# Residual by accumulating DMA, convolution in groups of eight, output stages by time

## The chip, the cores and the metric

The kernel runs on one core of a Trainium2 chip, as one launch. The metric is device time in microseconds, from the first to the last instruction; lower is better. A core has a matrix engine (PE, whose weight loads the profile lists apart as PEld), a vector engine (DVE), a scalar engine (ACT), a general engine (POOL), and SyncE (SP), which here only issues DMAs. POOL issues DMAs as well. PE writes to PSUM, which is cut into banks; DVE and ACT read PSUM and the on-chip memory SBUF; DMAs move data between SBUF and the main memory (HBM).

## The reference, cut to what matters

Two operations in a row: a depthwise convolution over seven past tokens, whose weights are a softmax for each of eight heads, and then a token-mixing block with a phase.

```python
# x: (8, 4224, 192); weight: (8, 7)
w = softmax(weight, axis=-1)
x = causal convolution of x along the tokens, w[h] for the 24 channels of head h

theta = x @ w_theta                       # 192 x 192
zr, zi = x * cos(theta), x * sin(theta)
yr = einsum('ts,bsd->btd', w_tok_r, zr)   # 4224 x 4224, mixes the tokens
yi = einsum('ts,bsd->btd', w_tok_i, zi)   # 4224 x 4224
u = x + yr + yi                           # the residual: x is the convolution's output
return u + np.maximum(u @ w_ch, 0.0)      # 192 x 192
```

## The kernel before

The tokens are 33 chunks `k` of 128 tokens on the input side of the token mixing, and 33 blocks `tb` of 128 tokens on its output side. A row holds batch times channel: N = 8 x 192 = 1536 elements.

**Steps.** The work on PE is a list of 58 steps. A step takes a pair of output blocks (the last unit has one block only) and at most NW = 11 chunks that are in SBUF as `z`. The two real products of a pair are done with seven matrix products instead of eight (sums and differences of weights and of `z` prepared by DVE). NU = 17 units of blocks pass by for each group of chunks, and partial sums go to `part` in HBM and come back 17 steps later. In the last 17 steps (`final`) the sum of a block is complete: the residual is added, and the output stage follows. In the last five of them, fewer than eleven chunks are left, so these steps are short.

```python
    # one step: seven runs over the chunks, two matmuls of 384 columns each time
    for r, (wn, zn, cn, opens, to) in enumerate(runs):
        if opens:
            y[cn] = ypool.tile([P, 2, PC], F32, name="y", tag="y")   # two PSUM buffers
        for c, k in enumerate(self.ks):
            while events and events[0][0] * len(runs) <= 7 * (r + c / self.n):
                events.pop(0)[1]()            # other work, placed in sevenths of the step
            yield k
            for q in range(2):
                pe(nc.tensor.matmul(y[cn][:, q, 0:BH], lhsT=..., rhs=chunks[k].z[...], ...))
        if to:
            self.give(y[cn], *to)             # DVE: pv += y
```

Every instruction of PE, DVE and ACT is kept in the order in which the program gives it.

**The convolution** of a chunk is four calls of `conv`, each for two heads: four matmuls into one PSUM bank (tile `pc`), which ACT copies into `z`. While the first eleven chunks are made, the calls stand in twos; afterwards each of them is an event of its own inside a step. Twenty-two chunks are made in that second way.

```python
        def conv(self, hp):
            ...
            pc = bank("pc")                   # one of four banks shared with v and tp
            for hh in range(2):
                h = 2 * hp + hh
                for half in range(2):
                    pe(nc.tensor.matmul(pc[half * 2 * Q : (half + 1) * 2 * Q, ...],
                        lhsT=bands[:, h, :, :]..., rhs=self.xw[:, half, :, ...]))
            act(nc.scalar.activation(out=self.x..., in_=pc[...], func=AT.Copy))
            # after the last call: DMAs of x, as f16 rows, to xs in HBM

        def tasks(self):
            for hp in range(4):
                yield lambda hp=hp: self.conv(hp)
            # then 2 transposes, 4 theta stages, 2 products, 2 sums
    ...
                # sevenths of the step for the tasks of one chunk
                pos = [0, .2, .4, .6, 1.3, 1.5, 2.1, 2.3, 2.5, 2.7, 3.1, 3.15, 3.4, 3.6]
```

**The residual** of a final step is loaded from `xs` and added by DVE to the partial sum `pv` in the step before.

```python
        def load_rows(self):
            for tb in self.tbs:
                pv = wk.tile([P, N], F32, name="pv", tag="big", bufs=6)
                if not self.first:
                    nc.sync.dma_start(out=pv, in_=part[(self.t // NU - 1) % 2][tb, :, :])
                self.pv.append(pv)

        def residual(self, i):
            xr = wk.tile([P, N], F16, name="xr", tag="xr", bufs=1)
            nc.sync.dma_start(out=xr, in_=xs[self.tbs[i] * P : (self.tbs[i] + 1) * P, :])
            dve(nc.vector.tensor_tensor(out=self.pv[i], in0=self.pv[i], in1=xr, op=ALU.add))
    ...
                    found.append((3.7 + 2.3 * i, lambda i=i: steps[t + 1].residual(i)))
```

**The output stage** of a block: ACT casts `pv` to f16 (`ub`), PE transposes it in two halves of six tiles (`tp`), ACT copies each half (`uT`), PE multiplies with `w_ch` (`v`, four times four matmuls), DVE does the maximum and the addition in place, and two DMAs take the result out. All of it stands in the next step, at places counted in sevenths of that step, whatever its length; after the last step it follows at once.

```python
        def outputs(self):
            for i in range(len(self.tbs)):
                at = 0.2 + 3.4 * i
                found.append((at, lambda i=i: self.cast(i)))          # 128 x 1536
                for g in range(NG):
                    found.append((at + 0.8 + 1.0 * g, lambda g=g: self.turn_u(g)))
                    for k in range(2):
                        found.append((at + 1.3 + 1.0 * g + 0.2 * k,
                                      lambda i=i, g=g, k=k: self.output(i, g, k)))
```

Of the kernel before, what the change touches and what calls it, by code (L numbers as in the profile page):

```python
# [9 lines left out]
AT = mybir.ActivationFunctionType  # L10
ALU = mybir.AluOpType
F16 = mybir.dt.float16
# [4 lines left out]
def kernel(  # L17
# [23 lines left out]
    nc = tc.nc  # L41
    B, S, D = x.shape
    H, KS = weight.shape
    G = D // H
    P = nc.NUM_PARTITIONS
    assert (B, D, P) == (8, 192, 128) and S % P == 0
    N = B * D
    HD = D // 2
    HN = N // 2
    NQ = 4  # L50
    Q = P // NQ
# [3 lines left out]
    WR = Q + HALO  # L55
    GB = 4
    NG = B // GB
    GC = GB * D
    BH = HN // 2
    NU = (NT + 1) // 2  # L60
    NW = 11
# [5 lines left out]
    NSTEP = start[-1] + NU  # L67
# [7 lines left out]
    def in_order(engine, ins):  # L75
        if engine in last:
            tc.add_manual_dep(ins.ins, last[engine].ins.name, NOSYNC, reason="order")
        last[engine] = ins
        return ins
# [4 lines left out]
    def dve(ins):  # L84
        return in_order("dve", ins)

    def act(ins):
        return in_order("act", ins)

    constp = ctx.enter_context(tc.tile_pool(name="const", bufs=1))  # L90
    wk = ctx.enter_context(tc.tile_pool(name="wk", bufs=2))
# [11 lines left out]
    xs = dram.tile([S, N], F16, name="xs")  # L103
    part = [dram.tile([NT, P, N], F32, name=f"part{i}") for i in range(2)]
# [26 lines left out]
    def channel_mix(tT, k, w):  # L131
        v = bank("v")
        for b in range(2):
            for i in range(2):
                pe(nc.tensor.matmul(  # L135
                    v[:, b * D : (b + 1) * D], lhsT=tT[:, 3 * k + b + i, :],
                    rhs=w[:, 2 * b + i, :], start=(i == 0), stop=(i == 1),
                ))
        return v[:, 0 : 2 * D]

    def transposed(u):
        tp = bank("tp", F16)
        for k in range(6):
            pe(nc.tensor.transpose(  # L144
                tp[:, k * P : (k + 1) * P], u[:, k * P : (k + 1) * P], ident
            ))
        uT = wk.tile([P, 6, P], F16, name="uT", tag="uT")
        act(nc.scalar.activation(  # L148
            out=uT[:, :, :].rearrange("p k s -> p (k s)"), in_=tp[:, 0 : 6 * P],
            func=AT.Copy,  # L150
        ))
        return uT
# [3 lines left out]
    class Chunk:  # L156
# [83 lines left out]

        def tasks(self):

            for hp in range(4):
                yield lambda hp=hp: self.conv(hp)
            for g in range(NG):
                yield lambda g=g: self.transpose(g)
            for g in range(NG):
                for k in range(2):
                    yield lambda g=g, k=k: self.theta(g, k)
            yield lambda: self.product(Z11)  # L250
            yield lambda: self.product(Z21)
            yield lambda: self.sums(0)
            yield lambda: self.sums(1)
# [13 lines left out]
    class Step:  # L267


        def __init__(self, t):  # L270
            self.t, self.u, self.ks = t, unit(t), active(t)
            self.n = len(self.ks)
            self.tbs = [tb for tb in (2 * self.u, 2 * self.u + 1) if tb < NT]
            self.pair = len(self.tbs) == 2
            self.first = t < NU
            self.final = t + NU >= NSTEP
            self.blocks = ("11", "21", "22", "12") if self.pair else ("11", "12")
            self.st, self.w, self.pv, self.xr = {}, {}, [], []

        def load_w(self, name):  # L280
            tb = self.tbs[int(name[0]) - 1]
# [52 lines left out]
                    )  # L334
                self.pv.append(pv)

        def residual(self, i):
            xr = wk.tile([P, N], F16, name="xr", tag="xr", bufs=1)
            nc.sync.dma_start(
                out=xr, in_=xs[self.tbs[i] * P : (self.tbs[i] + 1) * P, :]  # L340
            )
            dve(nc.vector.tensor_tensor(  # L342
                out=self.pv[i], in0=self.pv[i], in1=xr, op=ALU.add
            ))

        def give(self, y, i, h, copies):
            o = self.pv[i][:, :].rearrange(
# [55 lines left out]
                        out=part[(self.t // NU) % 2][tb, :, :], in_=self.pv[i]  # L403
                    )

        def cast(self, i):
            self.ub = wk.tile([P, N], F16, name="ub", tag="ub", bufs=1)
            act(nc.scalar.activation(out=self.ub, in_=self.pv[i], func=AT.Copy))  # L408

        def turn_u(self, g):  # L410
            self.uT = transposed(self.ub[:, g * GC : (g + 1) * GC])

        def output(self, i, g, k):
            pk = self.pv[i][:, g * GC + k * 2 * D : g * GC + (k + 1) * 2 * D]
            dve(nc.vector.scalar_tensor_tensor(  # L415
                out=pk, in0=channel_mix(self.uT, k, wch), scalar=0.0, in1=pk,
                op0=ALU.max, op1=ALU.add,
            ))
            if k == 1:
                rows = slice(self.tbs[i] * P, (self.tbs[i] + 1) * P)  # L420
                nc.sync.dma_start(
                    out=out[g * GB : (g + 1) * GB, rows, :].rearrange("b s d -> s b d"),
                    in_=self.pv[i][:, g * GC : (g + 1) * GC].rearrange(
                        "p (b d) -> p b d", d=D
                    ),
                )

        def outputs(self):
            found = []
            for i in range(len(self.tbs)):  # L430
                at = 0.2 + 3.4 * i
                found.append((at, lambda i=i: self.cast(i)))
                for g in range(NG):
                    found.append((at + 0.8 + 1.0 * g, lambda g=g: self.turn_u(g)))
                    for k in range(2):
                        found.append((at + 1.3 + 1.0 * g + 0.2 * k,
                                      lambda i=i, g=g, k=k: self.output(i, g, k)))
            return found

    steps = [Step(t) for t in range(NSTEP)]  # L440

    def step_events(t):
        found = []
        s = steps[t]
        if t + 1 < NSTEP:
            found += steps[t + 1].w_tasks()
            found.append((1.6, steps[t + 1].load_rows))
            if steps[t + 1].final:
                for i in range(len(steps[t + 1].tbs)):
                    found.append((3.7 + 2.3 * i, lambda i=i: steps[t + 1].residual(i)))  # L450
        if t + 2 < NSTEP:
            nxt = steps[t + 2]
            for j, name in enumerate(nxt.blocks):
                found.append(((0.3, 1.3, 2.3, 4.3)[j], lambda name=name: nxt.load_w(name)))
        if t > 0 and steps[t - 1].final:
            found += steps[t - 1].outputs()
        if t >= NU - 2:
            new = [k for k in range(NK) if start[k] == t + 2 and k >= NW]
            for k in new:
                found.append((4.5, lambda k=k: load_chunk(k)))  # L460
            at = 0.3
            for k in (k for k in range(NK) if start[k] == t + 1 and k >= NW):
                pos = [0, .2, .4, .6, 1.3, 1.5, 2.1, 2.3, 2.5, 2.7, 3.1, 3.15, 3.4, 3.6]

                def add(at, j, k):
                    def go():
                        if j == 0:
                            chunks[k].todo = chunks[k].tasks()
                        next(chunks[k].todo)()
                    found.append((at, go))  # L470
                for j, p in enumerate(pos):
                    add(at + p, j, k)
                at += 2.6
        return found
# [3 lines left out]
    spare = bank("spare")  # L478
    noise = zpool.tile([P, PC], F16, name="noise", tag="z")
    nc.vector.memset(noise, 0.0)  # L480
    masks = wk.tile([2 * WR, KS, 2, Q], F16, name="masks", tag="ub", bufs=1)
    nc.gpsimd.memset(masks, 1.0)
    for k in range(KS):
        nc.gpsimd.affine_select(
            out=masks[:, k, :, :], in_=masks[:, k, :, :], pattern=[[WR, 2], [1, Q]],
# [5 lines left out]
    for a, lo in ((0, True), (1, False)):  # L491
        nc.gpsimd.affine_select(
            out=block[:, a : a + 1], in_=block[:, a : a + 1], pattern=[[0, 1]],
# [6 lines left out]
        out=wsb, in0=wsb, in1=wmax[:, :].unsqueeze(2).to_broadcast([P, H, KS]),  # L500
        op=ALU.subtract,
# [10 lines left out]
        out=wbf, in0=wsb, in1=wrcp[:, :].unsqueeze(2).to_broadcast([P, H, KS]),  # L512
        op=ALU.mult,
# [2 lines left out]
    nc.vector.tensor_tensor(  # L516
        out=taps, in0=masks[:, :, 0, :], in1=masks[:, :, 1, :], op=ALU.add
    )
    btmp = wk.tile([2 * WR, 2, H, Q], F16, name="btmp", tag="xr", bufs=1)
    for k in range(KS):  # L520
        nc.vector.tensor_tensor(
            out=btmp[:, 1 if k else 0],
            in0=taps[:, k, :].unsqueeze(1).to_broadcast([2 * WR, H, Q]),
            in1=wbf[0 : 2 * WR, :, k].unsqueeze(2).to_broadcast([2 * WR, H, Q]),
            op=ALU.mult,
        )
        if k:
            nc.vector.tensor_tensor(
                out=btmp[:, 0], in0=btmp[:, 0], in1=btmp[:, 1], op=ALU.add
            )  # L530
    for a in range(2):
        nc.vector.tensor_scalar_mul(
            out=bands[:, :, a, :], in0=btmp[:, 0], scalar1=block[:, a : a + 1]
# [77 lines left out]
    wch = channel_weights(moe_w_ch, "wch")  # L611
    ready[0] = NK
    for _ in flow:
        pass
    for _, f in sorted(steps[-1].outputs(), key=lambda e: e[0]):
        f()


# [28 lines left out]
```

## Time and profile before

| | |
|---|---|
| time, median of 3 runs | 1490.7 us (1489.43 to 1496.38) |
| PE busy | 1448.0 us, 97% |
| DVE busy | 1034.9 us, 69% |
| ACT busy | 387.1 us, 26% |
| POOL busy | 566.9 us, 38% |
| moved by DMA | 268.99 MB, mean 180 GB/s |

How to read it: busy time is the union of the times in which an engine executes. Matmuls overlap in their pipeline, so the mean duration of one (327 ns for the large ones) is longer than the distance between the starts of two; how fast PE goes is read from starts, not from durations. A group's line gives the source line, engine, operation, the program's names, the shapes and the count, then busy time and mean ns, then the idle time of that engine just before, with what ended it. A line of the view by stages gives for a stretch its length, each engine's busy time and count of instructions, the granted clock of PE, the DMA share and GB/s.

The trace has five stretches: up to about 110 us the first eleven chunks are made; to 425 us there are steps alone; to 585 us the second eleven chunks are made beside the steps; to 880 us steps alone; to 1042 us the third eleven chunks; from there to the end are the final steps with their output stages.

### The profile page before, as it was taken

The page shows a single profiled execution, that of the slowest core. Times are in us where ns is not written, and L with a number is a line of the kernel's source. Part 1 is how long each engine was busy: PE and PEld are TensorE (multiplying, and loading weights), DVE is VectorE, ACT ScalarE, POOL GpSimd, SP SyncE. Part 2 cuts the span into 40 slices and gives each one's busy share as a digit, 9 for nine tenths or more (in the row PEclk, how much of TensorE's full clock was granted, in tenths as well). Part 3 has the DMA queues.
Part 4 walks back from the last instruction along what each step waited for, and adds up shares of the span by engine and source line. Part 5 has one row for each costly group of instructions (what it writes and reads, how often), then busy time and mean ns, then how long its engine had stood idle before and what let it go on. Part 6 is the DMA issues. An engine that isn't in the chain of part 4 may idle for free.

```text
span 1490.7 us, 25284 instructions
## 1 busy us (share of the span) xinstructions
PE 1448.0 (97%) x10083; PEld 899.1 (60%) x10083; DVE 1034.9 (69%) x1153; ACT 387.1 (26%) x631; POOL 566.9 (38%) x1054
## 2 busy tenths in 40 slices
PE   7899999999999999999999999998999999999996
PEld 3565666666665566666666656565666666666664
DVE  5884554545458777766657568778887787787885
ACT  6881101010134353000000025255112212121233
POOL 9753433332444542433333354442422322232320
PEclk9999999999999999999999999999999999999998
DMA  9996756565799998887878699999787887787783
GB/s 132 234 199 142 142 112 132 109 136 103 166 200 233 223 208 250 195 183 184 187 177 194 169 191 201 231 214 252 144 195 177 186 183 192 184 185 179 173 214 109
DMA packets 240023, 268.99 MB, mean 180 GB/s; under 512 B 76192, under 2 KB 209312, under 8 KB 239904
## 3 DMA queue, kind: packets, MB, share of 16 engines
q0 software_dynamic: 167232, 85.25, 46.9%
q1 hardware_dynamic: 72672, 182.12, 35.0%
q8 instruction: 79, 1.29, 0.3%
q14 instruction: 40, 0.33, 0.1%
HBM read 245.49 MB, written 101.06 MB: 232 GB/s over the span
## 4 chain that ended last, share of the span: by engine, by line
PE 86%; DMA 6%; POOL 3%; DVE 3%; issue 1%; ACT 1%; DVEq 0%; POOLq 0%; ACTq 0%
PE y L389 77%; PE v L135 5%; PE tp L144 2%; POOL st L287 2%; DMA st<-in_moe_w_tok_i_dram 2%; PE pc L190 2%; DMA xw<-in_x_dram 2%; DMA st<-in_moe_w_tok_r_dram 1%; DVE pv L354 1%; POOL xw L177 1%; DVE wt L299 1%; DMA xr<-xs 1%; DVE z L237 1%; DVE z L231 0%; ACT uT L148 0%
## 5 line engine op out<-in xcount | busy, mean ns | idle before, releaser
L389 PE MATMUL y<-z,wt 128*128 128x384 f16 x7656 | 1320.5, 327 | 17.1 <-DVE pv L354 12.0
L389 PEld LDWEIGHTS <-wt 128*128 128x128 f16 x7656 | 734.4, 98 | 473.9 <-issue 22.3
L354 DVE TENSOR_TENSOR pv<-y,pv 128x768 f32<-128x768 f32 x324 | 308.3, 952 | 362.4 <-PE y L389 361.7
L287 POOL DMA_DIRECT2D st<-in_moe_w_tok_r_dram x448 | 241.6, 548 | 425.9 <-DVE wt L299 390.8
L287 POOL DMA_DIRECT2D st<-in_moe_w_tok_i_dram x448 | 242.0, 549 | 404.5 <-DVE wt L299 366.5
L299 DVE STREAM_TRANSPOSE wt<-st 128x1408 f16<-128x1408 f16 (+7 forms) x224 | 326.5, 1462 | 10.0 <-DMA st<-in_moe_w_tok_r_dram 7.4
L148 ACT ACTIVATE uT<-tp 128x768 f16<-128x768 f16 x132 | 106.1, 818 | 330.3 <-PE tp L144 330.3
L311 DVE TENSOR_TENSOR wt<-wt 128x1408 f16<-128x1408 f16 (+7 forms) x216 | 173.4, 803 | 10.1 <-PE y L389 6.6
L197 ACT ACTIVATE z<-pc 128x384 f16<-128x384 f32 x132 | 63.3, 507 | 391.3 <-PE pc L190 390.2
L352 ACT ACTIVATE pv<-y 128x768 f32<-128x768 f32 x66 | 53.8, 817 | 275.6 <-PE y L389 274.7
L135 PEld LDWEIGHTS <-uT 128*128 128x128 f16 x1056 | 93.7, 99 | 40.8 <-ACT uT L148 9.9
L415 DVE SCALAR_TENSOR_TENSOR pv<-v,pv 128x384 f32<-128x384 f32 x132 | 71.2, 548 | 50.0 <-PE v L135 49.5
L177 POOL DMA_DIRECT2D xw<-in_x_dram x132 | 77.1, 602 | 38.8 <-DMA st<-in_moe_w_tok_r_dram 14.9
L226 ACT ACTIVATE z<-v,half_pi 128x384 f16<-128x384 f32 x132 | 77.8, 589 | 31.1 <-PE v L135 30.1
L237 DVE TENSOR_TENSOR z<-z 128x768 f16<-128x768 f16 x132 | 73.6, 557 | 4.8
L135 PE MATMUL v<-wch,uT 128*128 128x192 f16 x528 | 66.0, 251 | 6.4 <-ACT uT L148 6.4
L408 ACT ACTIVATE ub<-pv 128x1536 f16<-128x1536 f32 x33 | 48.8, 1480 | 65.9 <-DVE pv L354 65.9
L226 ACT ACTIVATE z<-v 128x384 f16<-128x384 f32 x132 | 65.5, 496 | 0.0
L231 DVE TENSOR_TENSOR z<-z 128x1536 f16<-128x1536 f16 x66 | 59.9, 949 | 7.7 <-ACT z L226 7.7
L135 PE MATMUL v<-wth,uT 128*128 128x192 f16 x528 | 61.8, 246 | 0.8 <-ACT z L226 0.8
L342 DVE TENSOR_TENSOR pv<-pv,xr 128x1536 f32<-128x1536 f32 x33 | 57.7, 1750 | 2.7 <-DMA xr<-xs 2.7
L190 PE MATMUL pc<-xw,bands 96*64 96x192 f16 x528 | 43.7, 256 | 3.3 <-DMA xw<-in_x_dram 2.8
(44 smaller groups left out, 180.3 us busy)
## 6 DMA issues: line engine op xcount, KB each, us to landing
part<-pv SPq DMA_DIRECT2D x79, 768.0 KB, 4.1
pv<-part SPq DMA_DIRECT2D x79, 768.0 KB, 5.8
out_dram<-pv SPq DMA_DIRECT2D x66, 384.0 KB, 3.9
st<-in_moe_w_tok_r_dram POOLq DMA_DIRECT2D x280, 88.0 KB, 4.9
st<-in_moe_w_tok_i_dram POOLq DMA_DIRECT2D x280, 88.0 KB, 3.4
xs<-z SPq DMA_DIRECT2D x132, 96.0 KB, 3.9
xr<-xs SPq DMA_DIRECT2D x33, 384.0 KB, 4.1
xw<-in_x_dram POOLq DMA_DIRECT2D x121, 96.0 KB, 4.9
```

Of the source, the lines that this page charges most:

```text
L135: pe(nc.tensor.matmul(v[:, b * D : (b + 1) * D], lhsT=tT[:, 3 * k + b + i, :], rhs=w[:, 2 * b + i, :], start=(i == 0), stop=(i == 1),))
L148: act(nc.scalar.activation(out=uT[:, :, :].rearrange("p k s -> p (k s)"), in_=tp[:, 0 : 6 * P], func=AT.Copy,))
L177: nc.gpsimd.dma_start(out=self.xw[lo : lo + n, h, :, :], in_=x[:, t0 : t0 + n, :].rearrange("b s d -> s b d"),)
L190: pe(nc.tensor.matmul(pc[half * 2 * Q : (half + 1) * 2 * Q, hh * B * G : (hh + 1) * B * G], lhsT=bands[:, h, :, :].rearrange("p a m -> p ( ...
L226: act(nc.scalar.activation(**args))
L237: dve(nc.vector.tensor_tensor(out=z[:, o, :], in0=z[:, a, :], in1=z[:, b, :], op=ALU.subtract))
L287: nc.gpsimd.dma_start(out=st[a * Q : (a + 1) * Q, :, 0:n], in_=w[tb * P : (tb + 1) * P, t0 : t0 + n] .rearrange("(bt i) s -> i bt s", bt=NQ),)
L299: dve(nc.vector.transpose(self.w[name][:, 0 : self.n, :, :], self.st[name][:, :, 0 : self.n * Q] .rearrange("p bt (c j) -> p c bt j", j=Q),))
L311: dve(nc.vector.tensor_tensor(out=self.w[name][:, 0 : self.n, :, :], in0=self.w[a][:, 0 : self.n, :, :], in1=self.w[b][:, 0 : self.n, :, : ...
L354: dve(nc.vector.tensor_tensor(out=o, in0=yv, in1=o, op=ALU.add))
L389: pe(nc.tensor.matmul(y[cn][:, q, 0:BH], lhsT=self.w[wn][:, c, :, :].rearrange("p bt i -> p (bt i)"), rhs=chunks[k].z[:, zn, q * BH : (q + ...
L415: dve(nc.vector.scalar_tensor_tensor(out=pk, in0=channel_mix(self.uT, k, wch), scalar=0.0, in1=pk, op0=ALU.max, op1=ALU.add,))
```

## The change

It has three parts.

1. The residual is added by the DMA itself: POOL issues a DMA from `xs` (f16) with an addition into the f32 target. For the final steps with all chunks the target is `pv` in SBUF, 1536 elements a row. For the five short steps (`late`) it is the partial sum in HBM, before it is loaded, in two DMAs of 768 elements a row. The program gives these four steps ahead. The loads of `xr` and the DVE additions go. The purpose is to take work off DVE and the loads out of the last steps.
2. In the steps, the four calls of `conv` stand as two groups of eight matmuls instead of four groups of four. The purpose is fewer changes of PE between kinds of matmul.
3. The output stages get places in microseconds of the main matmuls (0.324 us for a chunk and run) instead of sevenths of a step, and the cast is split in two halves, each ahead of its transposes. In the short steps the first block's output stage begins inside its own step, when its sum is complete after the sixth of seven runs. What falls after the last step is given in one order sorted by time, so that stages of several blocks are interleaved there. The purpose is that PE doesn't wait in the short last steps.

```diff
         def tasks(self):
-            for hp in range(4):
-                yield lambda hp=hp: self.conv(hp)
+            for hp in (0, 2):
+                yield lambda hp=hp: [self.conv(hp), self.conv(hp + 1)]
 ...
+            self.late = self.final and self.n < NW
+            self.time = 0.324 * self.n * (7 if self.pair else 4)
 ...
-        def residual(self, i):
-            xr = wk.tile([P, N], F16, name="xr", tag="xr", bufs=1)
-            nc.sync.dma_start(
-                out=xr, in_=xs[self.tbs[i] * P : (self.tbs[i] + 1) * P, :]
-            )
-            dve(nc.vector.tensor_tensor(
-                out=self.pv[i], in0=self.pv[i], in1=xr, op=ALU.add
-            ))
+        def add_x(self, i):
+            if self.late:
+                to = part[(self.t // NU - 1) % 2][self.tbs[i], :, :]
+            else:
+                to = self.pv[i]
+            rows = slice(self.tbs[i] * P, (self.tbs[i] + 1) * P)
+            for cols in (slice(0, HN), slice(HN, N)) if self.late else (slice(0, N),):
+                nc.gpsimd.dma_start(
+                    out=to[:, cols], in_=xs[rows, cols], accum_op=ALU.add
+                )
 ...
-        def cast(self, i):
-            self.ub = wk.tile([P, N], F16, name="ub", tag="ub", bufs=1)
-            act(nc.scalar.activation(out=self.ub, in_=self.pv[i], func=AT.Copy))
+        def cast(self, i, g):
+            self.ub[i, g] = wk.tile([P, GC], F16, name="ub", tag="ub", bufs=4)
+            act(nc.scalar.activation(
+                out=self.ub[i, g], in_=self.pv[i][:, g * GC : (g + 1) * GC], func=AT.Copy
+            ))
 ...
         def outputs(self):
             found = []
+            late = self.late and self.pair
             for i in range(len(self.tbs)):
-                at = 0.2 + 3.4 * i
-                found.append((at, lambda i=i: self.cast(i)))
+                at = ((-self.time / 7 + 0.6, 1.2) if late else (0.7, 12.7))[i]
+                cast, turn, mix = (1, 2.6, 4.4) if late else (2, 3.6, 5.4)
                 for g in range(NG):
-                    found.append((at + 0.8 + 1.0 * g, lambda g=g: self.turn_u(g)))
+                    d = at + (3 if late else 3.6) * g
+                    found.append((at + cast * g, lambda i=i, g=g: self.cast(i, g)))
+                    found.append((d + turn, lambda i=i, g=g: self.turn_u(i, g)))
                     for k in range(2):
-                        found.append((at + 1.3 + 1.0 * g + 0.2 * k,
+                        found.append((d + mix + 0.7 * k,
                                       lambda i=i, g=g, k=k: self.output(i, g, k)))
             return found
 ...
-            if steps[t + 1].final:
+            if steps[t + 1].final and not steps[t + 1].late:
                 for i in range(len(steps[t + 1].tbs)):
-                    found.append((3.7 + 2.3 * i, lambda i=i: steps[t + 1].residual(i)))
+                    found.append((3.3 + 1.7 * i, lambda i=i: steps[t + 1].add_x(i)))
+        if t + 4 < NSTEP and steps[t + 4].late:
+            for i in range(len(steps[t + 4].tbs)):
+                found.append((3.3 + 1.7 * i, lambda i=i: steps[t + 4].add_x(i)))
 ...
-                pos = [0, .2, .4, .6, 1.3, 1.5, 2.1, 2.3, 2.5, 2.7, 3.1, 3.15, 3.4, 3.6]
+                pos = [0, .5, 1.3, 1.5, 2.1, 2.3, 2.5, 2.7, 3.1, 3.15, 3.4, 3.6]
 ...
-    for _, f in sorted(steps[-1].outputs(), key=lambda e: e[0]):
-        f()
+    for at, f in sorted(outputs, key=lambda e: e[0]):
+        if at >= sum(s.time for s in steps):
+            f()
```

Two scratch tiles of the start (`masks`, `btmp`) move to the four buffers of `ub`, since the buffer of `xr` is gone.

More of the change, by code (lines that the diff above doesn't have):

```diff
@@ L276, in __init__ @@
             self.final = t + NU >= NSTEP
+            self.late = self.final and self.n < NW
+            self.time = 0.324 * self.n * (7 if self.pair else 4)
             self.blocks = ("11", "21", "22", "12") if self.pair else ("11", "12")
-            self.st, self.w, self.pv, self.xr = {}, {}, [], []
+            self.st, self.w, self.ub, self.uT, self.pv = {}, {}, {}, {}, []
         def load_w(self, name):
@@ L404, in mix, with turn_u @@
                     )
-        def cast(self, i):
-            self.ub = wk.tile([P, N], F16, name="ub", tag="ub", bufs=1)
-            act(nc.scalar.activation(out=self.ub, in_=self.pv[i], func=AT.Copy))
-        def turn_u(self, g):
-            self.uT = transposed(self.ub[:, g * GC : (g + 1) * GC])
+        def cast(self, i, g):
[3 more added lines that the diff above has]
+            ))
+        def turn_u(self, i, g):
+            self.uT[i, g] = transposed(self.ub[i, g])
         def output(self, i, g, k):
@@ L415, in output @@
             dve(nc.vector.scalar_tensor_tensor(
-                out=pk, in0=channel_mix(self.uT, k, wch), scalar=0.0, in1=pk,
+                out=pk, in0=channel_mix(self.uT[i, g], k, wch), scalar=0.0, in1=pk,
                 op0=ALU.max, op1=ALU.add,
@@ L440 @@
     steps = [Step(t) for t in range(NSTEP)]
+    outputs = [
+        (sum(s.time for s in steps[: t + 1]) + at, f)
+        for t in range(NSTEP) if steps[t].final for at, f in steps[t].outputs()
+    ]
     def step_events(t):
@@ L454, in step_events @@
                 found.append(((0.3, 1.3, 2.3, 4.3)[j], lambda name=name: nxt.load_w(name)))
-        if t > 0 and steps[t - 1].final:
-            found += steps[t - 1].outputs()
+        for at, f in outputs:
+            begin = at - sum(s.time for s in steps[:t])
+            if 0 <= begin < steps[t].time:
+                found.append((7 * begin / steps[t].time, f))
         if t >= NU - 2:
@@ L480 @@
     nc.vector.memset(noise, 0.0)
-    masks = wk.tile([2 * WR, KS, 2, Q], F16, name="masks", tag="ub", bufs=1)
+    masks = wk.tile([2 * WR, KS, 2, Q], F16, name="masks", tag="ub", bufs=4)
     nc.gpsimd.memset(masks, 1.0)
@@ L518 @@
     )
-    btmp = wk.tile([2 * WR, 2, H, Q], F16, name="btmp", tag="xr", bufs=1)
+    btmp = wk.tile([2 * WR, 2, H, Q], F16, name="btmp", tag="ub", bufs=4)
     for k in range(KS):
```

## The prediction

> **What bounds the kernel now.** I read the page first (shares of the engines, slices, groups), then the view by stages, then PE's own timeline where a stage is longer than its matmuls, then the waits.
>
> ```profile
> PE 1448.0 (97%) x10083; PEld 899.1 (60%) x10083; DVE 1034.9 (69%) x1153; ACT 387.1 (26%) x631; POOL 566.9 (38%) x1054
> PEclk9999999999999999999999999999999999999998
> ...
> L389 PE MATMUL y<-z,wt 128*128 128x384 f16 x7656 | 1320.5, 327 | 17.1 <-DVE pv L354 12.0
> ...
> L342 DVE TENSOR_TENSOR pv<-pv,xr 128x1536 f32<-128x1536 f32 x33 | 57.7, 1750 | 2.7 <-DMA xr<-xs 2.7
> ```
>
> PE is the bound: 97% busy at nearly the full clock. The 33 residual additions (57.7 us of DVE) are not on the path as such; they count only where PE waits for DVE.
>
> ```profile
> 425.00:585.00 160.00, 159.35 (x1223) 96.91 (x1221) 117.95 (x141) 79.24 (x153) 66.09 (x120) 1.00 1.00 226
> 585.00:880.00 295.00, 295.00 (x1819) 177.35 (x1816) 195.37 (x185) 1.17 (x3) 108.26 (x200) 1.00 0.80 183
> 1042.00:1340.00 298.00, 297.57 (x2121) 193.80 (x2121) 239.50 (x254) 59.39 (x58) 91.92 (x171) 0.99 0.80 182
> 1430.00:1460.00 30.00, 27.73 (x208) 18.29 (x207) 25.40 (x37) 9.22 (x10) 4.32 (x8) 0.94 0.70 190
> 1460.00:1491.00 31.00, 16.77 (x141) 12.03 (x139) 15.27 (x25) 10.70 (x11) 0.00 (x0) 0.82 0.32 102
> ```
>
> From 585 to 880 us there are main matmuls alone: 295 us / 1819 = 0.162 us each. From 1042 to 1340 a final step takes 29.0 us by the starts of its parts. Its own work is 11 chunks x 7 runs x 0.324 = 24.9 us, and two output stages of 24 transposes at 0.055 and 32 `v` matmuls at 0.0825 (from the starts in the trace), 4.0 us: 28.9 us. So these steps are already full, and splitting casts or thinning DVE cannot shorten them. I took the distance of every two matmul starts and subtracted the undisturbed one. What is left over: 23 us up to 110 us (the first chunks, untouched), 9 and 10 us in the two later convolution stages, 5.5 us just after 1042 us, and 22.5 us from 1430 us on. The change can only draw on the last three.
>
> **What the Trainium skill says.** "TensorE: Matmul & The Clock Gate", Back-to-back issue gap, gives N/2.4 + 2.5 ns for a warm matmul of N columns, 162.5 ns for 384; the trace agrees (0.162). The same page, Part 1 (the clock gate), says that after an idle window of about 3.4 us the array runs at half clock; the trace shows just that once (below). "DMA: Bandwidth & Descriptors", SWDGE vs HWDGE vs iDMA, says that an accumulating or casting DMA has to come from GpSimd, which fits where the change issues it. Its section SDMA does more than copy gives a most of 2048 elements for one accumulation; rows of 1536 and 768 are below it. No run here shows that figure yet, and no page gives the speed of such a DMA.
>
> **Part 1, groups of eight.** In the convolution stage PE goes back and forth:
>
> ```profile
> 452.28 0.82 PE L389 MATMUL y<-z,wt 128*128 128x384 f16 x4
> 453.03 0.36 PE L190 MATMUL pc<-xw,bands 96*64 96x192 f16 x4
> 453.32 0.82 PE L389 MATMUL y<-z,wt 128*128 128x384 f16 x4
> ...
> 78.06 0.52 PE L190 MATMUL pc<-xw,bands 96*64 96x192 f16 x8
> 78.52 1.15 PE L389 MATMUL y<-z,wt 128*128 128x384 f16 x6
> ```
>
> From 452.28 to 453.32 are 1.04 us: four main matmuls (0.65) and a group of four (0.39). Inside, pairs start 0.08 to 0.10 us apart, but the first starts 0.255 us after the main one before it (0.093 more than usual) and the next main one comes 0.179 after the last: entering and leaving cost more than the work. A group of eight, as the first chunks already have them beside main matmuls (78.06 to 78.52 = 0.46, plus the entry), adds up to 0.555 against 2 x 0.392 = 0.784. That is 0.229 us saved for each two groups. After 110 us the trace has 88 groups of four, hence 44 of eight: 44 x 0.229 = 10.1 us. Against it: two `pc` banks are now wanted at once out of four shared with `v` and `tp`, and where two chunks share a step, ACT (0.5 us for a bank, 1.1 for a `v`) may hold one; in the first chunks two groups have an extra 0.17 to 0.23 us in the middle. I take 1 us off: **-9 us**, all on the path, as PE is full there.
>
> **Part 2, the residual.** At the end of the third convolution stage DVE is late:
>
> ```profile
> 1035.66 1.75 DVE L342 TENSOR_TENSOR pv<-pv,xr 128x1536 f32<-128x1536 f32 x1
> 1037.33 1.82 DVE L231 TENSOR_TENSOR z<-z 128x1536 f16<-128x1536 f16 x2
> 1039.18 2.33 DVE L237 TENSOR_TENSOR z<-z 128x768 f16<-128x768 f16 x4
> 1041.43 0.95 DVE L354 TENSOR_TENSOR pv<-y,pv 128x768 f32<-128x768 f32 x1
> ...
> 1042.43 26.86 PE L389 MATMUL y<-z,wt 128*128 128x384 f16 x154 [3.62 <-DVE pv L354]
> ```
>
> DVE runs without a hole from 1032.46 on; the give that PE needs ends 3.6 us late, and ten matmul pairs or so after the stall run at half clock (granted 0.50 from 1043 to 1045), 1.6 us more; a stall of 0.7 us stands at 1035. Two residual additions (at 1029.66 and 1035.66, 3.5 us) lie in this queue, about what DVE is late by. Of 6 us lost I expect 5 back: **-5 us**. Elsewhere in the full steps the 57.7 us of DVE are worth nothing.
>
> The cost: 33 blocks go through accumulating DMAs. A 3072-byte packet takes 0.15 us and a 6144-byte one 0.27 us now. If a row needs the read of x, the read of the target and its write, partly side by side, my estimate is 0.4 to 0.5 us a row; 128 rows on 16 engines are 3 to 4 us a block, two blocks a step. Against the 1.2 us of the loads that go, the DMA share of a 29 us step rises from 0.80 to about 0.95. The convolution stages run at a share of 1.00 without harm, and the addition has some 10 us until the first give needs it. In the built order twelve of the eighteen late halves move up into the third convolution stage, which is already full of transfers. I put **+1 us** for this.
>
> **Part 3, the tail.** From 1430 us on PE loses 22.5 us, out of 60.7:
>
> ```profile
> PE v L135 <- ACT uT L148: 6.4, 8, 1.0
> PE tp L144 <- ACT ub L408: 2.9, 1, 2.9
> PE y L389 <- DVE pv L354: 2.2, 1, 2.2
> ```
>
> The waits at `y` (2.2 at 1451, with half clock after it about 3.5) come from a residual addition that waits 2.0 us for its load; these go. The waits for `uT` come from output stages squeezed into steps of 4 and 2 chunks, where the product follows its transposes with only two to four matmuls between. Six of them before the end of the main matmuls cost 5.5 us; 1.8 us of spacing and another block between should hide nearly all. So about 8 of 10.5 us lost before the last main matmul return. After it come now 13.8 us with one block to finish: give, cast, and twice the way through transposes, copy, product, addition, then 4 us of store. With the change some 3.5 us of PE work of the block pair before lies there too, between the last block's own steps; ACT (about nine instructions of 0.8) sets the pace, and I get about 15 us by adding up that chain. So the last main matmul comes 8 + 3.5 us earlier and the rest is about 1 us longer: **-10 us**.
>
> Sum: -9 - 5 + 1 - 10 = -23, that is 1490.7 - 23 = 1468 us.
>
> **Rivals.** (a) The accumulating DMA is slow, say twice my estimate: the share of a final step goes past 1, POOL, which issues in order, holds back the weight loads behind it, and PE waits for weights in twelve steps. For it: no run shows its speed, and POOL waits for landings already (27 us in the waits). Against it: weights are loaded a step ahead. It would make 1480 to 1500. (b) The tail is not released: with DVE busy 25.4 of 30 us there, gives come late and transposes placed at a fixed time after them wait; or the longer ACT chain at the end takes back the gain. The tail then gives 2 to 4 us: 1475. (c) Bank waits eat part 1: with four banks, groups of eight and two chunks in a step give 4 instead of 9: 1473. (d) All goes better: the tail's end is hidden down to give, one half's chain and store: 1461.
>
> **Range and chances.** The floor is near 1460: the tail's last chain of some 10 us cannot go, nor the first 110 us. Rivals (b) and (c) together make about 1480. So 1460 to 1481 for 8 in 10. Faster by over 2% means below 1460.9, only with (d): 0.12. Slower by over 2% needs (a) at its worst: 0.06. Within 2%: 0.82.
>
> **What would show it.** Right: groups of `pc` x8 in the stages at 425 and 880 us, these about 4.5 us shorter each; no stall of 3.6 us at the end of the third convolution stage; final steps still 29 us; PE's waits for `uT` before the last main matmul below 1.5 us. Wrong: final steps longer than 29.5 us, PE waiting for weights or for gives that wait for an accumulating DMA, `pc` groups split by waits for ACT, or over 17 us from the last main matmul to the end.

## The result and the profile after

The changed kernel takes 1481.0 us against 1490.07 us (medians on the same chip), a ratio of 0.993 with a 95% interval of 0.9901 to 0.996. That is 9 us, where 23 were predicted (1468 us). 1481 is also the upper end of the range that the prediction gave, but by luck: it was put there for rivals (b) and (c), and neither came true. First the page of the changed kernel:

```profile
PE 1435.6 (97%) x10083; PEld 902.6 (61%) x10083; DVE 980.7 (66%) x1120; ACT 385.9 (26%) x664; POOL 604.5 (41%) x1096
...
L394 PE MATMUL y<-z,wt 128*128 128x384 f16 x7656 | 1312.1, 327 | 24.7 <-DVE pv L359 19.7
```

DVE is 54 us less busy, nearly the 57.7 us of the additions. PE is 12 us less busy, in large part because it goes in and out of convolution groups half as often. But the main matmuls have waited longer for the gives of DVE (its additions of a finished product `y` to `pv`), 19.7 us instead of 12.0. The view by stages says where; first two stretches of the kernel before, then the changed kernel:

```profile
1020.00:1060.00 40.00, 35.87 (x247) 21.86 (x246) 37.38 (x39) 11.59 (x24) 16.55 (x31) 0.96 1.00 246
1060.00:1330.00 270.00, 270.00 (x1947) 176.81 (x1945) 215.42 (x230) 56.39 (x55) 78.62 (x147) 1.00 0.79 180
```

```profile
1020.00:1060.00 40.00, 26.83 (x157) 15.63 (x156) 22.77 (x27) 5.03 (x10) 15.09 (x26) 0.91 1.01 251
1060.00:1330.00 270.00, 270.00 (x1947) 176.84 (x1946) 185.22 (x213) 58.09 (x74) 104.28 (x175) 1.00 0.97 220
1430.00:1460.00 30.00, 30.00 (x246) 20.96 (x244) 23.47 (x38) 12.42 (x16) 4.29 (x8) 1.00 0.53 140
1460.00:1480.00 20.00, 11.86 (x117) 8.61 (x115) 11.78 (x19) 9.29 (x13) 0.00 (x0) 0.95 0.57 178
```

The full final steps are without a gap (270.00 of 270.00), although the DMA share has gone from 0.79 to 0.97 in that very stretch; the tail is now full up to 1460 us. At the end of the third convolution stage, from 1020 to 1060 us, PE stands still for 13 of 40 us, where it stood for 4 before. PE's timeline there has four stalls (in brackets the wait in us, and for whom):

```profile
1028.21 3.74 PE L394 MATMUL y<-z,wt 128*128 128x384 f16 x22 [2.06 <-DVE pv L359]
1033.98 5.41 PE L394 MATMUL y<-z,wt 128*128 128x384 f16 x22 [2.03 <-DVE pv L359]
1045.43 5.01 PE L394 MATMUL y<-z,wt 128*128 128x384 f16 x22 [6.04 <-DVE pv L359]
1053.48 2.76 PE L394 MATMUL y<-z,wt 128*128 128x384 f16 x16 [3.04 <-DVE pv L359]
```

DVE, which ran without a hole ahead of PE's stall before, now waits itself:

```profile
1024.54 1.22 DVE L237 TENSOR_TENSOR z<-z 128x768 f16<-128x768 f16 x2 [2.43 <-DMA xs<-z]
...
1044.42 0.96 DVE L359 TENSOR_TENSOR pv<-y,pv 128x768 f32<-128x768 f32 x1 [8.92 <-DMA st<-in_moe_w_tok_i_dram]
...
1052.46 0.96 DVE L359 TENSOR_TENSOR pv<-y,pv 128x768 f32<-128x768 f32 x1 [5.54 <-issue]
```

The two gives belong to the first final step, whose `pv` has to have its residual before; they set PE's third and fourth stall. The bracket of the first names a weight load, but a give reads no weights: of several waits the profile names the one that it saw last. By the landing times in the trace it was the residual: the two additions into `pv` landed at 1044.34 and 1052.39, each 0.1 us before its give. PE's first two stalls end with gives of the step before. The first of these stands behind a sum of `z` that had to wait 2.43 us until a DMA had read the rows of x that lay in its place (`xs<-z`), the second behind DVE's products and sums for the last chunks.

POOL's timeline shows when the addition into `pv` was issued at all:

```profile
1021.03 0.55 POOL L289 DMA_DIRECT2D st<-in_moe_w_tok_r_dram  x1 [3.19 <-DMA part<-xs]
1023.48 0.54 POOL L289 DMA_DIRECT2D st<-in_moe_w_tok_r_dram  x1 [1.90 <-DMA part<-xs]
1025.93 0.54 POOL L289 DMA_DIRECT2D st<-in_moe_w_tok_r_dram  x1 [1.91 <-DMA part<-xs]
...
1037.45 0.91 POOL L347 DMA_DIRECT2D pv<-xs  x1 [2.89 <-DMA st<-in_moe_w_tok_r_dram]
```

POOL gets one DMA out each 2.4 us. By the landing times each of these goes out 0.3 to 0.5 us after the landing of the DMA that POOL issued eight places before, and those are first late halves (`part<-xs`, the additions for the short steps), then weight loads behind them. The addition for the first final step had to wait for this weight load, which took 20 us to land (a line of the chain that ended last):

```profile
1016.68 20.22 DMA st<-in_moe_w_tok_r_dram
```

So it goes out at 1037.45 and lands 6.9 us later, about what such an addition takes (median 6.8 us on the page).

The following table is the method of the prediction, for all kernels: the distance between starts of successive matmuls, less the undisturbed one, in us. The columns are the second and third convolution stage (425 to 585 and 880 to 1010 us), its end (1010 to 1060), the full final steps (1060 to 1400), and all from 1400 us on with the last store. The column in brackets has PE's waits at that end alone; most of what the loss has beyond it is half clock after a stall, which some kernels got there and others did not (last section). Labels are those of the experiments below.

| kernel | convolution | its end | (waits in it) | full final | tail |
|---|---|---|---|---|---|
| before | 16.2 | 7.7 | (4.1) | 0.1 | 22.5 |
| changed | 7.4 | 17.4 | (13.2) | 0.1 | 9.5 |
| e1, groups of eight alone | 7.5 | 8.7 | (4.8) | 0.1 | 23.0 |
| e2, half rows added by DVE | 7.4 | 18.0 | (12.6) | 12.8 | 36.9 |
| e5, whole rows added by DVE | 7.4 | 5.8 | (4.8) | 0.1 | 17.3 |
| e3, adds in their place | 7.3 | 8.7 | (5.7) | 0.1 | 10.1 |
| e4, all adds into `pv` | 7.4 | 7.9 | (6.8) | 0.1 | 14.6 |
| e9, late adds with few bytes | 7.2 | 9.7 | (6.7) | 0.1 | 9.5 |
| e8, DMA adds alone | 16.2 | 11.6 | (7.1) | 0.1 | 18.7 |
| e7, first two steps early as well | 7.2 | 2.9 | (1.9) | 0.1 | 10.1 |

Changed against before: -8.8, +9.7 and -13.0 us, together -12; the stretch up to 425 us, with the same work, took 1 us more. So two parts brought 22 us, and the end of the third convolution stage took 10 of them back. (The first 110 us, with the same work in all ten kernels, lost up to 4 us more in one trace than in another; so the stages are compared here, and not only the totals.)

### The profile page after: what moved, and what is told of

Read it like the earlier page. It is cut to its first block, busy times and chain, and to the rows that moved or that the text cites. A ratio compares the mean times of both kernels' runs of the same rounds, so it can differ in the third digit from the quotient of the medians.

```text
span 1479.8 us, 25342 instructions
## 1 busy us (share of the span) xinstructions
PE 1435.6 (97%) x10083; PEld 902.6 (61%) x10083; DVE 980.7 (66%) x1120; ACT 385.9 (26%) x664; POOL 604.5 (41%) x1096
## 4 chain that ended last, share of the span: by engine, by line
PE 84%; DMA 9%; POOL 4%; DVE 2%; issue 1%; ACT 0%; SPq 0%; DVEq 0%; POOLq 0%; ACTq 0%
PE y L394 77%; PE v L135 4%; DMA xw<-in_x_dram 3%; DMA st<-in_moe_w_tok_r_dram 3%; PE tp L144 2%; POOL st L289 2%; DMA st<-in_moe_w_tok_i_dram 2%; PE pc L190 1%; DMA part<-xs 1%; POOL xw L177 1%; DVE pv L359 1%; DMA xw<-xw 0%; DMA part<-pv 0%; DVE z L237 0%; DVE z L231 0%
## 5 line engine op out<-in xcount | busy, mean ns | idle before, releaser
L394 PE MATMUL y<-z,wt 128*128 128x384 f16 x7656 | 1312.1, 327 | 24.7 <-DVE pv L359 19.7
L313 DVE TENSOR_TENSOR wt<-wt 128x1408 f16<-128x1408 f16 (+7 forms) x216 | 173.6, 804 | 10.1 <-PE y L394 6.6
L197 ACT ACTIVATE z<-pc 128x384 f16<-128x384 f32 x132 | 58.4, 504 | 384.2 <-PE pc L190 384.0
L413 ACT ACTIVATE ub<-pv 128x768 f16<-128x768 f32 x66 | 52.2, 835 | 71.8 <-DVE pv L359 71.7
L347 POOL DMA_DIRECT2D pv<-xs x24 | 22.1, 935 | 71.6 <-ACT ub L413 29.3
L190 PE MATMUL pc<-xw,bands 96*64 96x192 f16 x528 | 35.4, 254 | 4.4 <-DMA xs<-z 1.9
```

The source lines that it names most:

```text
L313: dve(nc.vector.tensor_tensor(out=self.w[name][:, 0 : self.n, :, :], in0=self.w[a][:, 0 : self.n, :, :], in1=self.w[b][:, 0 : self.n, :, : ...
L394: pe(nc.tensor.matmul(y[cn][:, q, 0:BH], lhsT=self.w[wn][:, c, :, :].rearrange("p bt i -> p (bt i)"), rhs=chunks[k].z[:, zn, q * BH : (q + ...
```

## The experiments

**e1: groups of eight alone.** The groups press the chunk work closer together, so they could have made the stall themselves.

```diff
-            for hp in range(4):
-                yield lambda hp=hp: self.conv(hp)
+            for hp in (0, 2):
+                yield lambda hp=hp: [self.conv(hp), self.conv(hp + 1)]
-                pos = [0, .2, .4, .6, 1.3, ...
+                pos = [0, .5, 1.3, ...
```

> The kernel before with the convolution groups of eight alone. If the groups give what the trace of the changed kernel shows in its convolution stages, 10 us come off: about 1480 us. If the stalls of the changed kernel around 1030 to 1053 us (16.5 us of lost PE time, where the kernel before lost 6) come from the groups of eight, which press the chunk work together, they stand here too and the time stays near 1488 to 1490 us.

1485.28 us against 1493.12 on that chip: ratio 0.9938 (0.9914 to 0.9963), 9 us by the ratio. The convolution stages lose 7.5 instead of 16.2 us, their end 8.7, with waits of 4.8 against 4.1 before. The groups give what was expected and do not make the stall.

**e2 and e5: the residual added by DVE, with the other two parts.** There was no room for the row of x beside four cast buffers, so e2 took half rows.

```diff
# e2, in place of add_x (cast buffers: bufs=3)
+            for cols in (slice(0, HN), slice(HN, N)):
+                xr = wk.tile([P, HN], F16, name="xr", tag="xr", bufs=1)
+                nc.sync.dma_start(out=xr, in_=xs[rows, cols])
+                dve(nc.vector.tensor_tensor(out=self.pv[i][:, cols],
+                    in0=self.pv[i][:, cols], in1=xr, op=ALU.add))
# e5: residual() of the kernel before, whole row (cast buffers: bufs=2)
```

> The changed kernel with the residual added by DVE again (x loaded in two halves of 768 elements, since the on-chip memory has no room for the whole row beside the new cast buffers; three cast buffers instead of four). Theory: the accumulating DMAs cost the 10 us at the end of the third convolution stage, so without them that stage loses about 6 us as before and the rest of the gain stays: 1468 to 1472 us, with some 2 us of waits for x in the last steps. Rival: the stalls have another cause (groups of eight, new places of the output stages): still 1479 to 1482 us.

1522.92 us, ratio 1.0196 (1.0162 to 1.0231): a miss of both forecasts. The waits of DVE in e2 (who waits for whom: total us, times, longest) show that it is no fair comparison:

```profile
DVE pv L345 <- DMA xr<-xs: 96.7, 33, 8.3
```

With one half-row buffer, the second half can be loaded only after the first is added, and DVE, in order, stands for the whole landing, 33 times. A whole row puts that right:

> As the run with DVE adding the residual, but with the whole row of x in one buffer, as in the kernel before, and two cast buffers. If the loss of that run (96.7 us of DVE waiting for x, half row by half row) came from its single half-row buffer, the full final steps are without a stall again and the sum is: groups of eight -10, end of the third convolution stage as before (about 8 us lost), tail 10 to 14 us lost instead of 22.5: 1468 to 1475 us. If DVE's adds do not fit with the new places of the output stages, the steps from 1060 us on lose several us here too: above 1485 us.

1475.71 us against 1491.36, ratio 0.9906 (0.989 to 0.9923), just above the 1468 to 1475 expected: the tail loses more than was thought. The full steps lose nothing again, so DVE's additions fit with the new places of the output stages. With the additions left on DVE the kernel is no slower than the changed one (0.993, 0.9901 to 0.996; the intervals overlap): as it stands, part 2 brings nothing. It gains 7.8 us in the tail (17.3 to 9.5, in part perhaps from the two cast buffers) and loses 11.6 at the end of the convolution, 8.4 of them in waits.

**e3: weight loads and adds of POOL in the program's order.** The program gives the late adds four steps ahead; twelve of eighteen stood in the third convolution stage (952.8 to 1014.0 us) because the scheduler moved them there, as soon as their data were complete. In e3 they are issued from 1279 to 1393 us.

```diff
+    def pool(ins):
+        return in_order("pool", ins)
...
-                nc.gpsimd.dma_start(out=to[:, cols], in_=xs[rows, cols], accum_op=ALU.add)
+                pool(nc.gpsimd.dma_start(out=to[:, cols], in_=xs[rows, cols], accum_op=ALU.add))
# the same around the DMAs of load_w
```

> The changed kernel with the weight loads and the residual adds of POOL kept in the order in which the program gives them, so that the late halves are added four steps ahead (1150 to 1300 us) and not, as the scheduler placed twelve of eighteen, in the third convolution stage. Theory: those twelve halves in a stage whose transfers are already full delay the weight loads and the first adds into pv behind them in POOL's queue; without them 7 to 11 of the 16.5 us lost there come back: 1470 to 1474 us. Rival: the adds into pv of the first two final steps wait for their own pv loads and are late by themselves: 1478 to 1481 us.

1472.99 us, ratio 0.9859 (0.9832 to 0.9887). The end of the convolution loses 8.7 instead of 17.4 us (waits 5.7 instead of 13.2), and the convolution, the full steps and the tail lose what they lose in the changed kernel. This is the theory's number: the hoisted halves cost 9 us. PE's timeline of e3 has three smaller stalls left, and POOL's and DVE's show when the first addition into `pv` goes out and what the second stall's give waits for:

```profile
1033.90 3.73 PE L397 MATMUL y<-z,wt 128*128 128x384 f16 x22 [1.90 <-DVE pv L362]
1040.05 5.41 PE L397 MATMUL y<-z,wt 128*128 128x384 f16 x22 [2.41 <-DVE pv L362]
1046.87 9.42 PE L397 MATMUL y<-z,wt 128*128 128x384 f16 x57 [1.41 <-DVE pv L362]
...
1026.05 0.90 POOL L350 DMA_DIRECT2D pv<-xs  x1 [0.24 <-DMA xs<-z]
...
1039.04 0.96 DVE L362 TENSOR_TENSOR pv<-y,pv 128x768 f32<-128x768 f32 x1 [3.63 <-DMA pv<-xs]
```

The addition goes out 11.4 us earlier than in the changed kernel and lands 12.9 us later (6.9 there), so it is there 5.4 us earlier. The longer waits for the two gives that need the additions (9.1 us in the changed kernel, 3.8 in e3) are thus a matter of the later issue alone: in the changed kernel the additions themselves land faster. The rest of the 9 us is the changed kernel's first stall of 2.1 us, which e3 does not have, and half clock.

**e4: every add into `pv`.** No late form at all, hence nothing that could be hoisted.

```diff
-            if self.late:
+            if False:
                 to = part[(self.t // NU - 1) % 2][self.tbs[i], :, :]
...
-            if steps[t + 1].final and not steps[t + 1].late:
+            if steps[t + 1].final:
```

> The changed kernel with every residual added into pv in SBUF one step ahead, none into the partial sums in HBM. Theory: as without the hoisted halves, 7 to 11 us come back at the end of the third convolution stage; the short last steps may lose 1 to 4 us, as their adds wait for pv loads: 1471 to 1477 us. Rival (the first adds into pv are late by themselves): 1479 to 1484 us.

1476.61 us, ratio 0.9887 (0.9842 to 0.9932). The end of the convolution loses 7.9 us, the tail 14.6 instead of 9.5. So the late form is worth 5 us in the short steps; its fault was only when it ran.

**e9: bytes or places?** The hoisted halves stand in POOL's queue, which issues in order, and they also fill the transfers. This kernel leaves out most of the residual of the last five steps: the late adds move 64 of 768 elements a row, in about the same places.

```diff
-            for cols in (slice(0, HN), slice(HN, N)) if self.late else (slice(0, N),):
+            for cols in (slice(0, 64), slice(HN, HN + 64)) if self.late else (slice(0, N),):
```

> The changed kernel with its late adds, twelve of which the scheduler again puts into the third convolution stage, cut to 64 of 768 elements a row; most of the residual of the last five steps is left out. POOL issues as many DMAs at about the same places, but hardly any bytes are moved by them. If the bytes in a stretch full of transfers cause the stall, the end of that stage loses 8 us or less, as with the adds in their place: 1470 to 1473 us. If the places in POOL's in-order queue cause it, 13 to 17 us stay lost there: 1477 to 1481 us.

1471.64 us, ratio 0.9846 (0.9813 to 0.9879); the end of the convolution loses 9.7 us (waits 6.7), a little over the 8 that the theory allowed, and far from the 13 to 17 of its rival. POOL's timeline of e9:

```profile
1024.87 0.93 POOL L347 DMA_DIRECT2D pv<-xs  x1 [0.24 <-issue]
```

With as many DMAs in the queue but few bytes, the first add into `pv` goes out 12.6 us earlier than in the changed kernel. So it is mostly the bytes. The twelve late halves took 10.2 us to land in the changed kernel (median) and 6.1 in e9; the weight loads issued just behind the last of them took 13 to 20 us and 4 to 8; and POOL waits for landings before it issues. The places in the queue account for about 1 us (9.7 against 8.7).

**e8: DMA adds alone, in their place, on the kernel before.** The prediction gave part 2 a gain of 5 us at the end of the convolution for the DVE time that it frees.

```diff
# before.py with add_x() in place of residual(), late adds four steps ahead,
# and pool() around add_x's and load_w's DMAs as in e3
```

> The kernel before with the accumulating DMAs alone, kept in their place in POOL's order; convolution groups and output stages as before. Theory: the DMA adds by themselves give only the residual wait of the tail back, 3 to 4 us, and change nothing at the end of the third convolution stage (8 us lost before and after): 1485 to 1488 us. Rival: taking 57.7 us from DVE frees the end of the convolution stage too: 1480 to 1483 us.

1491.77 us against 1491.36, ratio 0.9998 (0.9985 to 1.0011). A miss: 1485 to 1488 were expected. The tail gets 3.8 us back, as expected, but the end of the convolution loses 11.6 instead of 7.7 (waits 7.1 instead of 4.1). DVE is freed and then waits, in e8:

```profile
1043.60 0.96 DVE L361 TENSOR_TENSOR pv<-y,pv 128x768 f32<-128x768 f32 x1 [3.10 <-DMA pv<-xs]
...
1051.35 0.96 DVE L361 TENSOR_TENSOR pv<-y,pv 128x768 f32<-128x768 f32 x1 [5.24 <-issue]
```

A wait for DVE's 1.75 us additions has become a wait for the landing of the DMAs that took their place: by the trace they land at 1043.51 and 1051.27, each 0.1 us before its give.

**e7: the first two final steps early as well.** If that is so, these adds must not be made there at all. The rows of x that the first two final steps need come from chunks 0 to 15, complete long before; so e7 adds them into the partial sums in HBM eight steps ahead, among steps without convolution.

```diff
# on top of e3
+            self.early = self.final and t < NSTEP - NU + 2
...
-            if self.late:
+            if self.late or self.early:
                 to = part[(self.t // NU - 1) % 2][self.tbs[i], :, :]
...
+        if t + 8 < NSTEP and steps[t + 8].early:
+            for i in range(len(steps[t + 8].tbs)):
+                found.append((3.3 + 1.7 * i, lambda i=i: steps[t + 8].add_x(i)))
```

> The run with the adds in their place, and in addition the residual of the first two final steps added into the partial sums in HBM eight steps ahead, in the stretch without convolution. Theory: in the run with the adds in place the give of the first final step waits for an add that takes 12.9 us to land in a stretch full of transfers (waits of 2.4 and 1.4 us of PE, and half clock); with these adds gone from there, 3 to 6 us of the 8.7 us lost at that place come back: 1467 to 1470 us (ratio to before 0.983 to 0.986). Rival: DVE's own work (2.3 + 1.8 us of products and sums for the last chunks) sets that stall: 1472 to 1474 us.

1467.49 us against 1491.36, ratio 0.984 (0.9822 to 0.9858), the fastest of all. PE's timeline of e7 has one stall there, and the view by stages 38 of 40 us busy:

```profile
1033.05 23.24 PE L398 MATMUL y<-z,wt 128*128 128x384 f16 x142 [1.92 <-DVE pv L363]
```

```profile
1020.00:1060.00 40.00, 38.04 (x253) 23.59 (x252) 31.83 (x35) 7.80 (x16) 13.88 (x26) 1.00 0.82 187
```

The DMA share of this stretch is 0.82 (changed: 1.01), and PE keeps its full clock. What is left, 1.9 us, is DVE's own products and sums for the last chunks.

## Why the prediction was right and wrong

**Part 1, predicted -9.** Right: -8.8. All 44 groups are of eight and none is split for a bank; PE's timeline of the changed kernel:

```profile
452.52 0.52 PE L190 MATMUL pc<-xw,bands 96*64 96x192 f16 x8
452.98 1.80 PE L394 MATMUL y<-z,wt 128*128 128x384 f16 x10
454.71 0.52 PE L190 MATMUL pc<-xw,bands 96*64 96x192 f16 x8
```

From 452.52 to 452.98 are the 0.46 us that the prediction read off the first chunks. Rival (c), bank waits, did not occur.

**Part 3, predicted -10.** Right in the mechanism and 3 us too small: -13.0. The last main matmul starts at 1465.8 us instead of 1476.5, although what lies ahead of the tail is together 2 us longer: 12.7 us of it are the tail's own, where 11.5 were predicted. From there to the end it is 14.0 us instead of 14.1 (1 us more was predicted: the interleaved stages cost nothing on top). PE's waits for `uT` before the last main matmul, 4.5 us before, are gone, as the prediction asked. It is not the places alone: with the additions on DVE the tail loses 17.3 (e5), with the DMA adds and the old places 18.7 (e8), with both 9.5 to 10.1.

**Part 2, predicted -5 and +1.** This step failed: it measured +9.7. The prediction read a busy DVE queue just ahead of the stall and took the additions out of it, "about what DVE is late by". Of this 2.9 us came: in e3 PE waits 1.9 us for the last gives before the final steps, where e1 waits 4.8. But a give of a final step needs the residual, whoever adds it. DVE had added it before PE needed it, 1.75 us for a block after a load of 4 to 6 us; by DMA it lands in 12.9 us in that stretch (e3), and the two gives that wait for it cost PE 2.4 and 1.4 us. So even in their place the DMA adds save nothing there (waits of 5.7 us in e3 against 4.8 in e1 and e5). The 5 us were there to be had: e7, which makes the first additions earlier, loses 2.9 us at that place where e1 loses 8.7.

The +1 for the transfers was mis-sized: the prediction saw from the built order that twelve halves move up into the full stage, and let it pass because "the convolution stages run at a share of 1.00 without harm". From 880 to 1020 us the share went from 0.99 to 1.10, and POOL, which before had waited for free weight buffers, ahead of need, waited for landings instead:

```profile
POOL st L287 <- DVE wt L299: 46.6, 10, 9.8
```

```profile
POOL st L289 <- DVE wt L301: 7.6, 5, 2.6
```

(The first line is of the kernel before, 950 to 1050 us, the second of the changed one, 940 to 1045; waits for landings went from 7.7 us to about 40.) That took 9 us (e3). The share alone would not have told: e1, e3 and e9 stand at 1.03 to 1.05 in that stretch without such a loss. What the prediction could have asked is how long the landings ahead of the first consumer become, since POOL issues only as earlier transfers land.

**The speed of the addition** was right. By the trace's DMA records, a row of 1536 takes 0.37 us (median; 0.4 to 0.5 estimated) against 0.25 for a plain one of the same bytes, and the share of the full final steps 0.97 (0.95 predicted), without a stall: rival (a) as it was put, weights held back in twelve steps, did not come. Its mechanism did, in one stretch and with the parts exchanged: there additions into HBM and weight loads held back the additions into `pv`.

Open is why an addition in its place still takes 12.9 us to land at the end of the third convolution stage, where the median over the changed kernel is 6.8.

## What to carry to other kernels

Work that moves from a busy engine to a DMA does not leave the path if the consumer is near: it trades a duration for a landing time, here 12.9 us in a full stretch for 1.75 us of DVE (and a load made ahead). Look where a scheduler puts transfers that have no consumer for long; it may start them as soon as their data exist, in the fullest stretch, and pinning them to their place was worth 9 us of 1480. Where the operands exist early, do such additions in a stretch with slack, ahead of the crowded one (another 6 us of lost PE time, 1.6 of it half clock).

## What the runs showed of the hardware

A group of convolution matmuls (weights of 96 rows and 64 columns) among main ones (128 and 128) costs about 0.22 us for going in and out, whatever its length. From the start of the main matmul before to that of the one after are 0.545 us for a group of four (kernel before) and 0.710 for a group of eight (changed and e1); less the 0.162 of the main matmul that is 0.38 and 0.55 us, of which each four matmuls take 0.165.

Whether a stall brings half clock depends on how it lies in time. In each of the ten traces all changes of the granted clock lie on one grid of 3.41 us, and the spells of half clock last 3.41 us or a multiple (but for those that the end cuts off). I counted how long PE stood still in each such window of 3.41 us at full clock, from 110 us on. All 25 windows with 2.03 us or more were followed by half clock; of the rest, which go up to 2.01 us, only one was (1.82 us, in e7's tail). So the changed kernel lost its clock after a stall of 2.03 us that lay in one window, and e3 after one of 2.41. And e1 and e5 have the same stall of 3.62 us and the same busy time between 1020 and 1060 us, but not the same clock:

```profile
1020.00:1060.00 40.00, 35.18 (x206) 20.58 (x205) 33.45 (x34) 5.40 (x10) 11.80 (x22) 0.91 0.85 207
```

```profile
1020.00:1060.00 40.00, 35.17 (x226) 21.36 (x224) 35.24 (x34) 5.57 (x11) 13.27 (x25) 1.00 0.85 208
```

In e1 (first) 2.77 us of the stall lay in one window, and two windows of half clock followed; in e5 1.81 us lay in each of two, and none did. Their losses there, 8.7 and 5.8 us, differ by the 2.9 us of half clock. The prediction took an idle window of about 3.4 us as the condition and saw it met once in the kernel before; there half clock also began at 1452 us, after 2.2 us, and in the changed kernel 2.03 us of a window were enough.
